# Routing steps between attention pairs: moved into the burst of value products, some to GpSimd and ScalarE

## The chip, the cores and the metric

The kernel runs on one core of a Trainium2 chip. The metric is the device time of one launch in microseconds (us). Engines have these names: PE is TensorE (PEld its weight loads), DVE is VectorE, ACT is ScalarE, POOL is GpSimd, SP is SyncE, from whose queue most DMAs are issued. Each engine works through its own instructions in order and waits on semaphores of the others.

## The reference, cut to what matters

The output is attention, then a first mixture of experts that routes each token by its largest logit, then a second one with a fixed capacity. All the edits lie in the attention and in the first routing.

```python
q_n, k_n = rmsnorm(q, g_q), rmsnorm(k, g_k)            # batch 4, 12 heads, 448 rows, 64 wide
attn = exp(scores - rowmax)
attn = attn / (sum(attn) + 1e-09)
x = (attn @ v).transpose(0, 2, 1, 3).reshape(1792, 768)
logits = x @ w_gate + modality_bias[modality_id]       # 8 experts
e_idx = argmax(logits)
gate_w = max probability, denominator + 1e-09
out[e_idx == e] = gate_w * (relu(x @ w1[e]) @ w2[e])
```

## The kernel before, in words

**Attention as a pipeline of steps.** Two heads make a pair; there are 6 pairs to a batch and 24 in all, each of 8 steps (head h, block c of 112 query rows). `attention` is a loop over steps, and an order written out by hand: the engines run what the loop emits in that order. In a step, `s1` makes the scores of one block (two products into `sp`, L230 and L231) and DVE takes their negated row maximum `nm` (L232); `s1e` lets ACT take the exponential `e` and its row sum `sm` (L238); `s2`, three steps behind (LAG1 = 3), turns a block of `e` on PE into `tp` (L246) and copies it to `et` on ACT (L252), or on DVE (L249) for two blocks of eight. Once in a pair, in the step that the code calls the burst, `s3` runs the pair's 8 value products (16 matmul records of line L259, `op`). `s4` copies `op` to `ot` and takes the reciprocal `rs` of the row sums plus 1e-9 (L273, L274); `s5` turns the result back into rows and makes the gate logits (L286, into the bank `fpt`); `s6` scales them into `xp` (L294) and `ul` (L301). `xp` goes to DRAM as rows of `xs`.

The normed inputs of the next pair are prepared beside this: POOL squares and halves (`sq`, L110 and two L114, in two halves of a group, in pairs of odd number), DVE sums (L116), POOL takes the root (L140 to L143) and scales the rows (`xn`, L167), PE turns them into columns (`pt`, L188), ACT and DVE split them (`cut`, L192 to L199), SP copies them into `at` and `bt` (L205, L207) and POOL a part into `qz` (L209).

**Routing of a batch.** When a batch's last pair is done, `emit_batch` gives a generator: `choose` sums the logits over heads (`lg`, L583), adds the bias (L585), takes the maximum (`mx`, L588), the one-hot `oh` of the first maximum (lines L502 to L510, DVE), its bfloat16 copy `ohb` (L592), and the gate: `ex` (L595, exponential on ACT L597) and the values `tr` (L601 to L609). `place` multiplies `ohb` on PE with a triangle and ones (8 small products, L619 to L623, into `fpt`) and takes from them each token's place `pl` in its expert (L629 to L635). After the third batch `star` finds the fullest expert, SP loads its number, and the weights w1 of that expert are fetched (`raws`) and split. `drip()` stands behind most DVE instructions of a step and emits the next step of `drops` (root steps) or, if there is none, of `thin` (the routing generator): several routing steps a pipeline step.

**The first slot.** `slot0` (started in step K0 = 170) finds 128 tokens of the fullest expert, fetches their rows from `xs` with one indirect DMA (L1462, tile `x`), waits some steps and turns the six column blocks on PE (L1467), split by ACT and DVE (L1469, L1471). Their first products are `pg` (L969 to L971). `extra` holds one other DMA, of the routing table `l2` to `y` (L1477).

Of the kernel before, what the change touches and what calls it, by code (L numbers as in the profile page):

```python
# [10 lines left out]
F32 = mybir.dt.float32  # L11
F32R = mybir.dt.float32r
BF16 = mybir.dt.bfloat16
# [23 lines left out]
def attention(tc, q, k, v, g_q, g_k, w_gate, consts, qkv, hook, emit_pair, emit_batch, extra, nb=NB):  # L37
# [12 lines left out]
    with ExitStack() as ctx:  # L50
# [203 lines left out]
        def s3(i, kc):  # L254
# [3 lines left out]
            for h in range(2):  # L258
# [5 lines left out]
                    stop=kc == NC - 1,  # L264
                )

        def s4(i):
            b, j = pairs[i]
            st = state[i]
            st["ot"] = p2.tile([128, S], F32, name="ot")  # L270
            nc.scalar.activation(st["ot"], st["op"], AF.Copy)
            st["rs"] = rs = p2.tile([CP, 8], F32, name="rs")
            nc.vector.tensor_scalar(rs, st["sm"], 1e-9, None, op0=OP.add)  # L273
            nc.vector.reciprocal(out=rs, in_=rs)  # L274
            if j == 0:
                uls[b] = p2.tile([CP, NC, NH, E], F32, name="ul")
            st["xp"] = p2.tile([CP, NC, 128], F32, name="xp")

        def s5(i, half):
# [8 lines left out]
        def s6(i, half):  # L288
            b, j = pairs[i]
            st = state[i]  # L290
            xp, ul, fp = st["xp"], uls[b], st["fp", half]
            cc = slice(half * 2, half * 2 + 2)
            r4 = st["rs"][:, half * 4 : half * 4 + 4].rearrange("p (c h) -> p c h", h=2)
            nc.vector.tensor_tensor(  # L294
                out=xp[:, cc, :].rearrange("p c (h d) -> p c h d", h=2),
                in0=fp[:, :, 0:128].rearrange("p c (h d) -> p c h d", h=2),
                in1=r4.unsqueeze(3).to_broadcast([CP, 2, 2, D]),
                op=OP.mult,
            )
            drip()  # L300
            nc.vector.tensor_tensor(  # L301
                out=ul[:, cc, 2 * j : 2 * j + 2, :],
                in0=fp[:, :, 128:144].rearrange("p c (h e) -> p c h e", h=2),
                in1=r4.unsqueeze(3).to_broadcast([CP, 2, 2, E]),
                op=OP.mult,
            )
            drip()
            if half == 1:
                emit_pair(b, j, xp)
# [15 lines left out]

        def drip():

            for qu in drops, thin:
                if qu:
                    if next(qu[0], qu) is qu:  # L330
                        qu.pop(0)
                    break

        def chain(gen, step, marks):

# [34 lines left out]

        for step in range(8 * np_ + 16 + LAG1):
            i, t = divmod(step, 8)
            phase[0] = step
            if i < np_:
                if step == 1:
                    stats(1, 1, (3, 3), act=True)
                if step == 2:
                    while drops:
                        drip()
                    for x in (0, 1):  # L380
                        rows(1, x, nc.vector)
                if step == 16:
                    jobs.append(init)
                if t == 0:
                    start(i)
                    if i + 1 < np_:
                        late = 0 if i else 3
                        chain(cols(i + 1, 0), step + late, ((0, last), (1, first), (1, last)))
                        chain(cols(i + 1, 1), step + max(late + 1, CQ), ((0, last), (1, first), (1, last)))
                    if i % 2 and (i + 3) // 2 < len(groups):  # L390
                        stats((i + 3) // 2, step + 2, ST)
                t0 = 0 if i % 2 else 6
                if t in (t0, t0 + 1) and i + 2 < np_:
                    while t0 and drops:
                        drip()
                    rows(i + 2, t - t0)
                if t == (4 + LAG1) % 8 and i % 2 == (4 + LAG1) // 8 and i // 2 + 2 < len(groups):
                    load(i // 2 + 2)
            for g in first.pop(step, ()):
                next(g)  # L400
            i2, n2 = divmod(step - LAG1, 8)
            i3 = i2 - 1
            if 0 <= i3 < np_ and n2 == 4:
                s4(i3)
            if 0 <= i3 < np_ and n2 == HALF0 + 1:
                s6(i3, 0)
                if i3 == np_ - 1:
                    s6(i3, 1)
            if 0 < i3 < np_ and n2 == 1:
                s6(i3 - 1, 1)  # L410
            burst = 0 <= i3 < np_ and n2 == (1 if i3 == np_ - 1 else BURST)
            if i < np_:
                s1(i, t)
                if burst:
                    s1e(i, t)
            if burst:
                for kc in range(NC):
                    s3(i3, kc)
            if 8 * np_ <= step < 8 * np_ + FILLED:
                for _ in range(FILL):  # L420
                    nc.tensor.matmul(spare()[:, 128:384], lhsT=consts["ones"], rhs=consts["ones"].unsqueeze(1).to_broadcast([128, 2, 128]), start=True, stop=True)
            if 0 <= i2 < np_:
                s2(i2, n2)
            if i < np_ and not burst:
                s1e(i, t)
            if step < 8 + LAG1:
                warm(nc, consts, idle, 6 if step < 3 else 3)
            if step < 2:
                for _ in range(3):
                    drip()  # L430
            if 0 <= i3 < np_ and n2 == HALF0:
                s5(i3, 0)
                if i3 == np_ - 1:
                    s5(i3, 1)
            if 0 < i3 < np_ and n2 == 0:
                s5(i3 - 1, 1)
            for g in last.pop(step, ()):
                drip()
                next(g)
            drip()  # L440
            job = extra(step)
# [8 lines left out]


LAG1 = 3
BURST = 3
WARM = 88
LEFT = 16
# [4 lines left out]
EV_DVE = (1, 4)  # L460
EV_LAST = (1, 4, 5, 7)
ST = (3, 5)
HALF0, FREE = 5, (3, 4)
CQ = 3


# [48 lines left out]
class Router:  # L515
# [61 lines left out]
    def choose(self, b, ul):  # L577
# [4 lines left out]
        lg = pool.tile(shp, F32, name="lg")  # L582
        nc.vector.tensor_reduce(out=lg, in_=ul.rearrange("p c h e -> p c e h"), axis=AX.X, op=OP.add)  # L583
        yield
        nc.vector.tensor_tensor(out=lg, in0=lg, in1=self.bt[:, js, :], op=OP.add)  # L585
        yield
        mx = pool.tile([CP, NC], F32, name="mx")
# [3 lines left out]
        self.ohb = self.pool.tile(shp, BF16, name="ohb")  # L591
        nc.vector.tensor_copy(out=self.ohb, in_=oh)  # L592
        yield
        ex = pool.tile(shp, F32, name="ex")
        nc.vector.tensor_tensor(out=ex, in0=lg, in1=mx.unsqueeze(2).to_broadcast(shp), op=OP.subtract)  # L595
        yield
        nc.scalar.activation(ex, ex, AF.Exp)  # L597
        yield
        yield
        gs = pool.tile([CP, NC], F32, name="gs")  # L600
        nc.vector.tensor_reduce(out=gs, in_=ex, axis=AX.X, op=OP.add)  # L601
        yield
        nc.vector.tensor_scalar(gs, gs, 1e-9, None, op0=OP.add)
        yield
        nc.vector.reciprocal(out=gs, in_=gs)
        yield
        nc.vector.tensor_copy(out=self.tr[:, js, 1], in_=gs)
        yield
        nc.vector.tensor_tensor(out=self.tr[:, js, 2], in0=gs, in1=self.tr[:, js, 1].bitcast(F32), op=OP.subtract)  # L609
        yield  # L610

    def place(self, b, pc, free=None):
# [17 lines left out]
        nc.vector.tensor_tensor(out=nxt, in0=pc[:, w : w + E], in1=cur, op=OP.add)  # L630
        self.n += 1
        yield
        nc.vector.tensor_tensor(out=ps, in0=ps, in1=self.oh[:, js, :], op=OP.mult)
        yield
        nc.vector.tensor_reduce(out=self.pl[:, js], in_=ps, axis=AX.X, op=OP.add)  # L635
# [781 lines left out]
def front(tc, consts, rp, q, k, v, g_q, g_k, modality_id, w_gate, bias, xs, w1, w2, wt, qkv, x0, l2, y):  # L1417
# [6 lines left out]
    with ExitStack() as ctx:  # L1424
# [8 lines left out]
            st["r"] = Router(tc, consts, rp, rwork, modality_id, bias, xs)  # L1433
            return st["r"].init()

        def pair(b, j, xp):
            st["r"].store(b, j, xp)

        def batch(b, ul):
            r = st["r"]  # L1440
            yield from r.choose(b, ul)
# [17 lines left out]
        def slot0():  # L1459
            r = st["r"]  # L1460
            yield from r.first_slot(st["p"][:, : 4 * (NB - 1)])
            nc.gpsimd.indirect_dma_start(out=xg, out_offset=None, in_=xs[: (NB - 1) * S], in_offset=IndirectOffsetOnAxis(ap=r.slot0[0][:, 0:1], axis=0))  # L1462
            for _ in range(5):
                yield
            for c in range(KD):
                px = (st["spare"]() if c % 2 else st["p"])[:, :128]
# [5 lines left out]
                yield  # L1472
# [1051 lines left out]
```

## Time and profile before

| what | value |
|---|---|
| median of 3 runs | 1006.93 us (1005.2 to 1008.8) |
| the profiled execution | 1000.97 us, its span 999.3 us |
| mean granted TensorE clock | 0.987 |
| busy PE, PEld | 961.2 us (96%), 778.4 us (78%) |
| busy DVE, ACT, POOL | 672.2 us (67%), 504.3 us (50%), 301.2 us (30%) |
| chain that ended last | PE 31%, issue 2%, DMA 1%, DVE 1%, ACT 1% |

Busy shares are of the span; idle time of PE is what is left of 100%. A row of a timeline has the start, the time, engine, line and operation, the tile written and the tiles read, the count, and in square brackets how long the engine was idle before it and who ended that. [...]

### The profile page before, as it was taken

The page shows a single profiled execution, that of the slowest core. Times are in us where ns is not written, and L with a number is a line of the kernel's source. Part 1 is how long each engine was busy: PE and PEld are TensorE (multiplying, and loading weights), DVE is VectorE, ACT ScalarE, POOL GpSimd, SP SyncE. Part 2 cuts the span into 40 slices and gives each one's busy share as a digit, 9 for nine tenths or more (in the row PEclk, how much of TensorE's full clock was granted, in tenths as well). Part 3 has the DMA queues.
Part 4 walks back from the last instruction along what each step waited for, and adds up shares of the span by engine and source line. Part 5 has one row for each costly group of instructions (what it writes and reads, how often), then busy time and mean ns, then how long its engine had stood idle before and what let it go on. Part 6 is the DMA issues. An engine that isn't in the chain of part 4 may idle for free. (4 is left out here: it accounts for less than half of the span.)

```text
span 999.3 us, 19414 instructions
## 1 busy us (share of the span) xinstructions
PE 961.2 (96%) x6241; PEld 778.4 (78%) x6241; DVE 672.2 (67%) x1742; ACT 504.3 (50%) x1128; POOL 301.2 (30%) x431
## 2 busy tenths in 40 slices
PE   7999999999989999999999999899999999999996
PEld 6766667677655688888888889756767699999996
DVE  6687877877875655545474665586788887787660
ACT  5787778778775422222362122561223475576651
POOL 4777667666633130001062101100010011210100
PEclk9899999999999999999999999999999999999998
DMA  6577566567465326446641111007751386866631
GB/s 164 139 156 167 138 156 165 134 159 175 112 171 194 104 90 261 144 176 222 224 165 51 33 33 66 20 15 278 256 208 37 111 303 206 270 199 237 217 122 31
DMA packets 81039, 152.58 MB, mean 153 GB/s; under 512 B 14270, under 2 KB 53438, under 8 KB 80768
## 3 DMA queue, kind: packets, MB, share of 16 engines
q1 hardware_dynamic: 75376, 127.63, 42.8%
q0 software_dynamic: 5200, 23.33, 7.2%
q8 instruction: 54, 0.88, 0.4%
q14 instruction: 89, 0.73, 0.3%
q10 hardware_dynamic: 320, 0.00, 0.0%
HBM read 112.27 MB, written 17.44 MB: 130 GB/s over the span
## 5 line engine op out<-in xcount | busy, mean ns | idle before, releaser
L238 ACT ACTIVATE e<-sp,nm 112x448 f32<-112x448 f32 x192 | 123.4, 643 | 46.4 <-DVE nm L232 43.0
L232 DVE TENSOR_REDUCE nm<-sp 112x1 f32<-112x448 f32 x192 | 116.1, 617 | 44.9 <-PE sp L231 44.4
L246 PEld LDWEIGHTS tp<-ident,e 112*112 112x112 f32 x768 | 87.7, 136 | 42.4 <-ACT et L252 9.9
L1056 DVE CUSTOM_DVE_ANT_0 prod<-po,wgb,gt 128x384 bf16<-128x384 f32 x96 | 92.7, 965 | 37.8 <-ACT yr L1280 34.3
L246 PE MATMUL tp<-ident,e 112*112 112x112 f32 x768 | 109.2, 265 | 6.6 <-ACT et L252 6.6
L2271 PE MATMUL bank<-xx,w1h 128*128 128x448 f32 x288 | 92.5, 378 | 0.0
L252 ACT ACTIVATE et<-tp 112x448 f32<-112x448 f32 x142 | 78.3, 551 | 26.7 <-PE tp L246 26.7
L230 PE MATMUL sp<-bt,at 128*112 128x448 f32 x188 | 83.9, 446 | 0.9 <-DMA bt<-cut 0.9
L969 PE MATMUL pg<-w1h,xh 128*128 128x512 f32 x180 | 75.0, 417 | 4.4 <-ACTq L926 2.2
L992 PE MATMUL po<-w2h,hh 128*128 128x384 f32 x224 | 78.9, 352 | 0.1
L259 PE MATMUL op<-et,qkv 112*64 112x448 f32 x384 | 79.0, 554 | 0.0
L2272 PE MATMUL bank<-xx,w1l 128*128 128x224 f32 x288 | 76.5, 266 | 0.0
L2311 POOL DMA_INDIRECT out_dram<-x,ids x16 | 16.4, 1026 | 198.6 <-ACT x L2310 150.2
L993 PE MATMUL po<-w2l,hh 128*128 128x384 f32 x224 | 75.2, 336 | 0.1
L994 PE MATMUL po<-w2h,hl 128*128 128x384 f32 x224 | 75.2, 336 | 0.0
L970 PE MATMUL pg<-w1l,xh 128*128 128x512 f32 x180 | 71.3, 396 | 0.0
L971 PE MATMUL pg<-w1h,xl 128*128 128x512 f32 x180 | 71.2, 395 | 0.0
L231 PE MATMUL sp<-bt,qz 128*112 128x448 f32 x188 | 70.5, 375 | 0.0
L2303 PE MATMUL bank<-w2h,hh 128*112 128x384 f32 x192 | 66.3, 345 | 0.0
L2305 PE MATMUL bank<-w2h,hl 128*112 128x384 f32 x192 | 64.7, 337 | 0.0
L2304 PE MATMUL bank<-w2l,hh 128*112 128x384 f32 x192 | 64.7, 337 | 0.0
L1092 POOL DMA_INDIRECT y<-yr,ti x11 | 11.4, 1038 | 161.6 <-POOLq L926 119.6
(476 smaller groups left out, 2289.2 us busy)
## 6 DMA issues: line engine op xcount, KB each, us to landing
qkv<-in_moe_w_dram SPq DMA_DIRECT2D x88, 384.0 KB, 4.6
qkv<-in_moe_w_dram SPq DMA_DIRECT2D x36, 512.0 KB, 8.3
raw<-in_moe_w_dram SPq DMA_DIRECT2D x24, 512.0 KB, 6.0
bt<-cut SPq DMA_DIRECT2D x96, 112.0 KB, 2.3
at<-cut SPq DMA_DIRECT2D x96, 112.0 KB, 2.3
w1s<-in_moe_w_dram SPq DMA_DIRECT2D x12, 512.0 KB, 6.9
w2s<-in_moe_w_dram SPq DMA_DIRECT2D x16, 384.0 KB, 8.2
qkv<-in_v_dram SPq DMA_DIRECT2D x12, 448.0 KB, 6.6
```

Of the source, the lines that this page charges most:

```text
L230: nc.tensor.matmul(sp, lhsT=at[:, h, cs], rhs=bt[:, h, :], start=True, stop=False)
L232: nc.vector.tensor_reduce(out=st["nm"][:, n : n + 1], in_=sp, axis=AX.X, op=OP.max, negate=True)
L238: nc.scalar.activation(e, st.pop(("s", n)), AF.Exp, bias=st["nm"][:, n : n + 1], accum_out=st["sm"][:, n : n + 1])
L246: nc.tensor.transpose(tp[:, kc, :], e[:, kc * CP : (kc + 1) * CP], ident[:CP, :CP])
L252: nc.scalar.activation(dst, tp, AF.Copy)
L259: nc.tensor.matmul(st["op"][h * D : (h + 1) * D, :], lhsT=raws[i // 2][:, 2, 2 * (i % 2) + h, kc * D : (kc + 1) * D], rhs=st["et"][:, h, k ...
L992: nc.tensor.matmul(po[n], lhsT=hh[:, k, :], rhs=w2h[:, kk, cs], start=kk == 0, stop=False)
L993: nc.tensor.matmul(po[n], lhsT=hh[:, k, :], rhs=w2l[:, kk, cs], start=False, stop=False)
L994: nc.tensor.matmul(po[n], lhsT=hl[:, k, :], rhs=w2h[:, kk, cs], start=False, stop=kk == KF - 1)
L1056: nc.vector.tensor_tensor_reduce(out=prod, in0=y, in1=wgb[:, cs, e], scale=gt, scalar=init[:, e : e + 1] if init is not None else 0.0, op0 ...
L2271: nc.tensor.matmul(pg, lhsT=h[:, k, fs], rhs=xx[:, k].rearrange("p a c -> p (a c)"), start=k == 0, stop=False)
L2272: nc.tensor.matmul(pg[:, :CAP], lhsT=l[:, k, fs], rhs=xh[:, k, :], start=False, stop=k == KD - 1)
```

## The change

- Routing steps of `thin` are no longer emitted by `drip()` while pairs run. `trickle()` emits one at the end of each step, and five in the burst step, behind the value products.
- The bias stands in `ul` as a thirteenth head (copied there by POOL, `fill`), so the sum over heads includes it and its own addition is gone. `ul` has one buffer.
- For the first three batches `ohb` is made by ACT, `ex` by POOL; the gate's later steps are a generator of their own, `gate`, which waits QUIET = 5 steps, with its constant on ACT and `tr` on POOL. The places are multiplied and summed on POOL (`fold`, three additions). The last batch keeps DVE.
- `place` may emit its products in one phase of eight (FREE) and not two.
- The row sums' constant is added by ACT in the burst step (`totals`), for every pair, and DVE takes the reciprocal alone.
- The turning of the first slot's rows begins 9 steps (LANDS) behind the gather, not 5, and takes two steps a block, not three. The DMA of the routing table is emitted in step 37, not 33.

```diff
+        def totals(i):
+            st = state[i]
+            st["rs"] = p2.tile([CP, 8], F32, name="rs")
+            nc.scalar.activation(st["rs"], st["sm"], AF.Copy, bias=1e-9)
+
         def s4(i):
...
-            st["rs"] = rs = p2.tile([CP, 8], F32, name="rs")
-            nc.vector.tensor_scalar(rs, st["sm"], 1e-9, None, op0=OP.add)
-            nc.vector.reciprocal(out=rs, in_=rs)
+            nc.vector.reciprocal(out=st["rs"], in_=st["rs"])
             if j == 0:
-                uls[b] = p2.tile([CP, NC, NH, E], F32, name="ul")
+                uls[b] = p2.tile([CP, NC, NH + 1, E], F32, name="ul", bufs=1)
...
-            for qu in drops, thin:
+            for qu in (drops, thin) if phase[0] >= 8 * np_ else (drops,):
...
+        def trickle():
+
+            if thin and phase[0] < 8 * np_ and next(thin[0], thin) is thin:
+                thin.pop(0)
...
             if burst:
+                totals(i3)
                 for kc in range(NC):
                     s3(i3, kc)
+                for _ in range(THIN):
+                    trickle()
...
             drip()
+            trickle()
...
+QUIET, THIN, LANDS = 5, 5, 9
...
-HALF0, FREE = 5, (3, 4)
+HALF0, FREE = 5, (4,)
...
+    def fill(self, b, ul):
+
+        self.tc.nc.gpsimd.tensor_copy(out=ul[:, :, NH, :], in_=self.bt[:, b * NC : (b + 1) * NC, :])
...
-        nc.vector.tensor_tensor(out=lg, in0=lg, in1=self.bt[:, js, :], op=OP.add)
...
+        if b == NB - 1:
+            nc.vector.tensor_copy(out=self.ohb, in_=oh)
+            yield
+            nc.vector.tensor_tensor(out=ex, in0=lg, in1=mxb, op=OP.subtract)
+            yield
+            yield from self.gate(b, ex, nc.vector)
+            return
+        nc.scalar.activation(self.ohb, oh, AF.Copy)
+        nc.gpsimd.tensor_tensor(out=ex, in0=lg, in1=mxb, op=OP.subtract)
+        jobs.append(self.gate(b, ex, nc.gpsimd, QUIET))
+        yield
...
+        if b < NB - 1:
+            nc.gpsimd.tensor_tensor(out=ps, in0=ps, in1=self.oh[:, js, :], op=OP.mult)
+            self.fold(self.pl[:, js], ps)
+            yield
+            return
...
-            for _ in range(5):
+            for _ in range(LANDS):
                 yield
...
                 nc.vector.tensor_tensor(out=xl[:, c, :], in0=px, in1=xh[:, c, :].bitcast(F32), op=OP.subtract)
-                yield
...
-            if i == 33:
+            if i == 37:
```

The order of the instructions at three places follows. The first is DVE's order from the step before the burst to the step behind it, when the first batch is routed; `req`, `rtm` and `oh` are the steps of the one-hot. Before:

```order
L232 TENSOR_REDUCE nm<-sp 112x1
L504 TENSOR_TENSOR req<-req,er 112x32
L507 TENSOR_REDUCE rtm<-req 112x4
L116 TENSOR_REDUCE ss<-sq 112x2x8
L510 TENSOR_TENSOR oh<-req,rtm 112x32
L232 TENSOR_REDUCE nm<-sp 112x1
L592 CAST ohb<-oh 112x32
L595 TENSOR_TENSOR ex<-lg,mx 112x32
L273 TENSOR_SCALAR rs<-sm 112x8
L274 RECIPROCAL rs<-rs 112x8
L232 TENSOR_REDUCE nm<-sp 112x1
```

And now the same steps of DVE in the changed kernel:

```order
L232 TENSOR_REDUCE nm<-sp 112x1
L116 TENSOR_REDUCE ss<-sq 112x2x8
L613 TENSOR_REDUCE mx<-lg 112x4
L232 TENSOR_REDUCE nm<-sp 112x1
L515 TENSOR_TENSOR req<-lg,mx 112x32
L517 TENSOR_TENSOR req<-req,er 112x32
L520 TENSOR_REDUCE rtm<-req 112x4
L523 TENSOR_TENSOR oh<-req,rtm 112x32
L277 RECIPROCAL rs<-rs 112x8
L232 TENSOR_REDUCE nm<-sp 112x1
```

The row maximum of the burst step stands ahead of the one-hot now, and the four steps of the one-hot stand together behind it; the copy `ohb`, `ex` and the constant of `rs` have left DVE.

The second place is ACT's order at the same burst; `e` twice are the exponentials of the two steps that end with the burst step. Before:

```order
L238 ACTIVATE e,sm<-sp,nm 112x448 x2
L252 ACTIVATE et<-tp 112x4x112
L271 ACTIVATE ot<-op 128x448
L597 ACTIVATE ex<-ex 112x32
L238 ACTIVATE e,sm<-sp,nm 112x448
```

And now on ACT:

```order
L238 ACTIVATE e,sm<-sp,nm 112x448 x2
L270 ACTIVATE rs<-sm 112x8
L623 ACTIVATE ohb<-oh 112x32
L252 ACTIVATE et<-tp 112x4x112
L276 ACTIVATE ot<-op 128x448
L238 ACTIVATE e,sm<-sp,nm 112x448
```

Two instructions have come in between the exponentials and the copy `et`, and the second of them reads what DVE makes last in the burst.

The third place is PE's order around the products of `place` for the same batch, which read `ohb`. Before, they stood at the end of the following burst step, ahead of the value products:

```order
L246 MATMUL tp<-ident,e 112x112 x4
L230 MATMUL sp<-bt,at 112x448
L231 MATMUL sp<-bt,qz_135 112x448
L619 LDWEIGHTS ut
L619 MATMUL fpt<-ohb,ut 128x32
```

And now on PE:

```order
L259 MATMUL op<-et,qkv_86 64x448 x8
L246 MATMUL tp<-ident,e 112x112 x4
L230 MATMUL sp<-bt,at 112x448
L231 MATMUL sp<-bt,qz_136 112x448
L246 MATMUL tp<-ident,e 112x112 x4
L658 LDWEIGHTS ut
L658 MATMUL fpt<-ohb,ut 128x32
```

They stand one step behind the burst in which the one-hot is made, ahead of that step's successor's score products.

## Rows read from the trace of the kernel before

**Rows 1.** Stretches from burst to burst, and the rest behind attention
```profile
96.28:107.67 11.39, 11.39 (x82) 8.31 (x81) 8.35 (x19) 9.64 (x28) 7.51 (x9) 1.00 0.92 222
72.31:84.81 12.50, 11.61 (x81) 8.33 (x80) 8.38 (x19) 10.02 (x28) 7.54 (x9) 1.00 1.07 210
107.67:123.29 15.62, 13.50 (x89) 9.75 (x88) 14.05 (x38) 9.87 (x28) 10.89 (x21) 0.89 0.35 80
180.96:196.46 15.50, 13.38 (x89) 9.91 (x89) 14.12 (x38) 9.79 (x28) 10.77 (x21) 0.89 0.35 84
254.13:268.42 14.29, 12.17 (x89) 8.51 (x88) 13.61 (x37) 9.31 (x27) 9.64 (x19) 1.00 0.37 84
350.00:975.00 625.00, 617.01 (x3911) 525.28 (x3910) 409.74 (x1055) 252.80 (x479) 90.50 (x104) 1.00 0.46 158
```

**Rows 2.** Waits of PE from 20 to 350 us: total, times, longest
```profile
PE tp L246 <- ACT et L252: 6.6, 4, 2.1
PE fpt L1467 <- DMA x<-xs,xi: 3.4, 1, 3.4
PE pg L969 <- ACT e L238: 1.3, 1, 1.3
PE sp L230 <- DMA bt<-cut: 0.9, 1, 0.9
```

**Rows 3.** Timeline of DVE from 106.5 to 116 us
```profile
109.57 0.18 DVE L502 TENSOR_TENSOR req<-lg,mx 112x32 f32<-112x32 f32 x1
...
110.20 1.35 DVE L504 TENSOR_TENSOR req<-req,er 112x32 f32<-112x32 f32 x1
111.59 0.19 DVE L507 TENSOR_REDUCE rtm<-req 112x4 f32<-112x32 f32 x1
111.69 0.41 DVE L116 TENSOR_REDUCE ss<-sq 112x16 f32<-112x256 f32 x1
112.02 0.89 DVE L510 TENSOR_TENSOR oh<-req,rtm 112x32 f32<-112x32 f32 x1
112.83 0.61 DVE L232 TENSOR_REDUCE nm<-sp 112x1 f32<-112x448 f32 x1
```

**Rows 4.** Timeline of POOL in the same pair
```profile
109.61 1.90 POOL L110 TENSOR_TENSOR sq<-qkv 112x1024 f32<-112x1024 f32 x1
111.59 2.07 POOL L114 TENSOR_TENSOR sq<-sq 112x512 f32<-112x512 f32 x2
```

**Rows 5.** Timeline of ACT in the same pair
```profile
113.54 0.64 ACT L238 ACTIVATE e<-sp,nm 112x448 f32<-112x448 f32 x1 [2.43 <-DVE nm L232]
...
114.16 0.53 ACT L252 ACTIVATE et<-tp 112x448 f32<-112x448 f32 x1
...
115.01 0.24 ACT L597 ACTIVATE ex<-ex 112x32 f32<-112x32 f32 x1
```

**Rows 6.** Timeline of PE: the stall of the same pair
```profile
114.75 0.60 PE L246 MATMUL tp<-ident,e 112*112 112x112 f32 x4 [2.12 <-ACT et L252]
```

**Rows 7.** Timeline of PE behind a burst without routing
```profile
96.28 3.23 PE L259 MATMUL op<-et,qkv 112*64 112x448 f32 x16
...
100.59 0.44 PE L230 MATMUL sp<-bt,at 128*112 128x448 f32 x1
```

**Rows 8.** Timeline of DVE in a pair without routing, burst at 84.81
```profile
86.81 0.42 DVE L116 TENSOR_REDUCE ss<-sq 112x16 f32<-112x256 f32 x1 [1.26 <-POOL sq L114]
...
87.68 0.98 DVE L273 TENSOR_SCALAR rs<-sm 112x8 f32<-112x8 f32 x1
```

**Rows 9.** Timeline of PE at the gathered rows
```profile
296.76 0.30 PE L1467 MATMUL fpt<-ident,x 128*128 128x128 f32 x1 [3.44 <-DMA x<-xs,xi]
...
297.52 4.73 PE L259 MATMUL op<-et,qkv 112*64 112x448 f32 x16
```

**Rows 10.** The tile bt from 285 to 310 us: its DMA issues and their landing
```profile
L205 SPq DMA_DIRECT2D bt<-cut x4: 462/530/876, 294.3 to 296.9; - x4
...
DMA to landing us min/median/max: 4.6/5.2/5.6
```

More of the change, by code (lines that the diff above doesn't have):

```diff
@@ L308, in s6 @@
             if half == 1:
-                emit_pair(b, j, xp)
+                emit_pair(b, j, xp, ul)
                 del state[i]
@@ L575, in store, with fold, choose @@
         self.tc.nc.sync.dma_start(out=self.xs[b * S : (b + 1) * S, 128 * j : 128 * j + 128].rearrange("(p c) d -> p c d", c=NC), in_=xp)
-    def choose(self, b, ul):
+    def fill(self, b, ul):
+        self.tc.nc.gpsimd.tensor_copy(out=ul[:, :, NH, :], in_=self.bt[:, b * NC : (b + 1) * NC, :])
+    def fold(self, out, x):
+        eng, t = self.tc.nc.gpsimd, self.work.tile([CP, NC, E // 2], F32, name="fold")
+        eng.tensor_tensor(out=t, in0=x[:, :, : E // 2], in1=x[:, :, E // 2 :], op=OP.add)
+        eng.tensor_tensor(out=t[:, :, 0:2], in0=t[:, :, 0:2], in1=t[:, :, 2:4], op=OP.add)
+        eng.tensor_tensor(out=out, in0=t[:, :, 0], in1=t[:, :, 1], op=OP.add)
+    def choose(self, b, ul, jobs):
         nc, pool, c = self.tc.nc, self.work, self.c
@@ L582, in choose @@
         lg = pool.tile(shp, F32, name="lg")
+        ex = pool.tile(shp, F32, name="ex")
+        mx = pool.tile([CP, NC], F32, name="mx")
+        mxb = mx.unsqueeze(2).to_broadcast(shp)
+        self.ohb = self.pool.tile(shp, BF16, name="ohb")
         nc.vector.tensor_reduce(out=lg, in_=ul.rearrange("p c h e -> p c e h"), axis=AX.X, op=OP.add)
         yield
-        nc.vector.tensor_tensor(out=lg, in0=lg, in1=self.bt[:, js, :], op=OP.add)
-        yield
-        mx = pool.tile([CP, NC], F32, name="mx")
         nc.vector.tensor_reduce(out=mx, in_=lg, axis=AX.X, op=OP.max)
@@ L590, in choose, with gate @@
         oh = yield from first_max_onehot_steps(nc, pool, lg, mx, c["er"], "r", out=self.oh[:, js, :])
-        self.ohb = self.pool.tile(shp, BF16, name="ohb")
-        nc.vector.tensor_copy(out=self.ohb, in_=oh)
-        yield
-        ex = pool.tile(shp, F32, name="ex")
-        nc.vector.tensor_tensor(out=ex, in0=lg, in1=mx.unsqueeze(2).to_broadcast(shp), op=OP.subtract)
-        yield
+        if b == NB - 1:
[8 more added lines that the diff above has]
+        jobs.append(self.gate(b, ex, nc.gpsimd, QUIET))
+        yield
+    def gate(self, b, ex, eng, wait=0):
+        nc = self.tc.nc
+        js = slice(b * NC, (b + 1) * NC)
+        for _ in range(wait):
+            yield
         nc.scalar.activation(ex, ex, AF.Exp)
         yield
-        yield
-        gs = pool.tile([CP, NC], F32, name="gs")
+        gs = self.work.tile([CP, NC], F32, name="gs")
         nc.vector.tensor_reduce(out=gs, in_=ex, axis=AX.X, op=OP.add)
         yield
-        nc.vector.tensor_scalar(gs, gs, 1e-9, None, op0=OP.add)
+        if eng is nc.vector:
+            nc.vector.tensor_scalar(gs, gs, 1e-9, None, op0=OP.add)
+        else:
+            nc.scalar.activation(gs, gs, AF.Copy, bias=1e-9)
         yield
@@ L606, in choose @@
         yield
-        nc.vector.tensor_copy(out=self.tr[:, js, 1], in_=gs)
+        eng.tensor_copy(out=self.tr[:, js, 1], in_=gs)
         yield
-        nc.vector.tensor_tensor(out=self.tr[:, js, 2], in0=gs, in1=self.tr[:, js, 1].bitcast(F32), op=OP.subtract)
+        eng.tensor_tensor(out=self.tr[:, js, 2], in0=gs, in1=self.tr[:, js, 1].bitcast(F32), op=OP.subtract)
         yield
@@ L1434, in hook, with pair @@
             return st["r"].init()
-        def pair(b, j, xp):
+        def pair(b, j, xp, ul):
             st["r"].store(b, j, xp)
+            if j == NPAIR - 2:
+                st["r"].fill(b, ul)
         def batch(b, ul):
             r = st["r"]
-            yield from r.choose(b, ul)
+            yield from r.choose(b, ul, st["q"])
             if b < NB - 1:
@@ L1471, in slot0 @@
                 nc.vector.tensor_tensor(out=xl[:, c, :], in0=px, in1=xh[:, c, :].bitcast(F32), op=OP.subtract)
-                yield
         def extra(i):
-            if i == 33:
+            if i == 37:
                 nc.sync.dma_start(out=y[:, DM:].rearrange("(c p) e -> p c e", p=128), in_=l2[:, :NT, :])
```

## The prediction, made before the change was run

> **What bounds the kernel now.** I read the table of stretches first, then PE's waits, then the timelines at the longest of them. Behind attention PE is busy 617.0 of 625 us at full clock [rows 1]: whatever attention gives up earlier should arrive at the end, since the work there follows PE and not the clock on the wall. Inside attention an undisturbed pair takes 11.39 us and PE is busy for all of it [rows 1], so DVE, ACT or POOL instructions gain nothing by being shorter unless a wait of PE hangs on them. The waits are few [rows 2]: `tp` on `et`, 6.6 us in 4 waits; the first slot's gather, 3.4; `pg`, 1.3; and `bt`, 0.9.
>
> The pairs in which a batch is routed take 15.62, 15.50 and 14.29 us [rows 1]. In the first, DVE is behind: it reaches the row maximum of the burst step at 112.83 [rows 3], which ends at 113.44; ACT, idle for 2.43, begins the exponential at 113.54 and the copy `et`, queued behind it, at 114.16 [rows 5]; PE gets its bank back at 114.75 after 2.12 us idle [rows 6]. [...]
>
> **What makes DVE late.** L502 takes 0.18 us; L504, the same size, takes 1.35, and L510 0.89 [rows 3]. L504 ends at 111.55, just after POOL's square, which ends at 111.51; L510 ends at 112.91, inside the two halvings that run from 111.59 to 113.66 [rows 4], so the first halving ends there. A sum over the same stretch, L116, took 0.41 beside POOL. So an addition or comparison of two SBUF tiles, and also L273, which took 0.98 beside POOL [rows 8], waits for POOL's running instruction; reductions don't. [...]
>
> **Routing, part by part.** All times are from the burst's start B (107.67 in the first batch). Removed from DVE are the bias addition, `ohb`, `ex`, the constant of `rs` and the `tr` steps. The row maximum of the burst step now stands ahead of the one-hot. But two things stand in the way of reading this as the end of the stall. POOL's squares are where they were, B+1.94 to B+3.84, then the halvings from B+3.92 to B+5.99 with the first ending about B+5.2 [rows 3, 4]. And `ohb` is on ACT ahead of `et`, while PE's `place` products stand one step behind the burst. PE reaches them when it would have reached the next score product, at 100.59 - 96.28 = B+4.31 [rows 7].
>
> DVE: L116 still waits for POOL to B+2.00 (86.81 - 84.81) and ends at B+2.42 [rows 8]; `mx`, which overlaps it, and the maximum of 0.61 [rows 3] end about B+3.1. The first comparison asks then and is held to the end of the square, B+3.88, as L504 was. The product with `er` comes next, at B+3.92: at that very moment POOL starts its halving (L507, which stood in that place, and L114 both start at 111.59 [rows 3, 4]). I take it that DVE, whose request follows at once, gets through: B+4.1; `rtm` B+4.3; `oh` is held until the first halving ends, B+5.24 as L510 was. ACT starts 0.10 later (113.44 to 113.54) and takes about 0.24 (the nearest row is the exponential of the same size), PE follows 0.06 later (114.69 to 114.75) [rows 3, 5, 6]: B+5.64. PE's wait is 5.64 - 4.31 = 1.33 in place of 2.12, a gain of 0.79, three times: 2.4 us. A wait of 0.9 left no trace on the clock (the pair of 12.50 us is at 1.00 [rows 1]), one of 2.12 did in two of three cases; at 1.33 I expect no fall and add the 2.5. Queued behind `ohb` on ACT are `et` and `ot`; PE needs `et` only after `place` and a score product, 0.9 us later, so they cost nothing more. Bounds for the three stalls: from nothing gained (below) to all 6.4.
>
> Edits at nothing: the constant of `rs` on ACT (24 small instructions) lies in the burst, where ACT is idle between the exponentials and `et`; it is idle 1.75 of 11.39 us in a clean pair [rows 1], and if that cover were gone PE would be late by about 0.2 a pair. POOL's `fill`, `ex`, product, three additions and two `tr` steps are eight small instructions a batch, at the 0.24 of ACT's small one [rows 5] 2 us, on an engine idle 3.88 of 11.39 us [rows 1]; queued behind most of them are the scaled rows of the pair after the next, which can wait. At a halving's 1.04 each (2.07 / 2 [rows 4]) they would be 8.3, and those rows could come up to 4 us late a batch: I take the first, since the size is that of the small one. The removal of L273's 0.98 shortens nothing in a clean pair, since PE did not wait there.
>
> **The first slot.** The gather's wait is 3.44 us, and the burst behind it takes 4.73 us in place of 3.23 at the lower clock [rows 7, 9]: 4.94. Four steps later, behind the burst, the rows (there at 296.7 [rows 9]) are met at about 300.5, so this wait goes. What is late next is the last pair's `bt`: its four DMAs are issued from 294.3 to 296.9 and land 4.6 to 5.6 us later, about 300.1 for the two that the first score product reads [rows 10]. Without the stall the burst is at 297.52 - 3.44 = 294.08 and that product at 294.08 + 4.31 = 298.4. I put a new wait of 1.7 there; bounds 0 (they land before they are wanted) and 2.5 (all four wanted). Net 3.2.
>
> **The table's DMA** goes from ahead of `bt` to behind it. The wait of 0.9 stands in just that pair, which took 12.50 against 11.39 [rows 1, 2]; I count 0.9, bounds 0 and 1.1. `pg` waits 1.3 for a bank behind a late exponential [rows 2] and is now emitted about one turn and some filler later: 0.6, bounds 0 and 1.3.
>
> **Sum:** 2.4 + 2.5 + 3.2 + 0.9 + 0.6 = 9.6. The profiled execution would go from 1000.97 to 991.4; it lies 6.0 below the median of the runs, so the forecast in their measure is 1006.93 - 9.6 = 997.3.
>
> **Rivals.**
> 1. *POOL wins the tie.* The product with `er` is then held to B+5.24, `rtm` ends at B+5.47, `oh` is held to the end of the second halving, B+6.04, and PE starts `place` at B+6.44: a wait of 2.13, the old stall under another name, with the old clock. What stays is 3.2 + 0.9 + 0.6 = 4.7: 1002.2. For it: the start times are equal to a hundredth. Against it: L502, asked for while POOL was about to go from one instruction to the next, was through in 0.18, POOL's next one starting at 109.61 [rows 3, 4]. [...] Chance 0.30 against 0.48.
> 2. *The stall goes altogether*, if DVE's steps all pass between POOL's instructions: 6.4 + 2.5 + 4.7 = 13.6, 993.3. Against it: L504 and L510 were both held. Chance 0.10.
> 3. *The gain is not handed on*, because something behind attention is bound by transfers or by a chain off PE: about 1006. Against it: 617.0 of 625 and a DMA share of 0.46 [rows 1]. Chance 0.07.
> 4. *Slower: ACT and PE are tied to DVE.* If one more POOL square (1.90) falls ahead of the one-hot, `ohb` holds ACT's `et` and PE in all three batches: waits of 4.0 in place of 2.12, 5.7 us, and the clock falls behind the third too, 1.3. Less 4.7 that is 2.3 over: 1009. It decides from a PE wait of 3.3 us; with the slot's new wait at its upper end and a fall of the clock there it comes to about 1011.5. Against it: POOL's queue in front of the burst is unchanged. Chance 0.05.
>
> **How the numbers follow.** What a measurement can tell from no change is 0.3%, 3.0 us. The forecast and the second rival lie beyond it (0.48, 0.10, less 0.01), the first rival mostly (0.26 of 0.30): faster 0.83. The rest of the first rival, the third and a little of the fourth: same 0.12; slower 0.05. The forecast's own range is 994.5 to 1000 (routing 1.5 to 3.5, slot 2.4 to 4.9). For 8 in 10 it has to take in most of the first rival and stop short of the second's centre: 993 to 1004.
>
> **What would show it.** Right: in the three routing pairs PE waits for `ohb` by ACT, about 1.3 us, ahead of `place`, and no longer for `et`; `oh` and the first comparison on DVE are long (0.9 each) and the product with `er` short; the granted clock of those pairs is 1.00. The gather's wait is gone and a wait for `bt` or `at` of 1 to 2 us stands behind that burst; the pair with the table's DMA is about 11.5 us. Wrong: the product with `er` over 1 us (first rival); no wait of PE at `place` (second); pairs as forecast but a stretch behind 350 us longer by as much (third); waits above 3.3 us (fourth).

## The result and the profile after

The changed kernel took 992.42 us (median of 6, 990.62 to 996.66), the kernel before beside it 1005.30 (6 runs): ratio 0.9883, 95% interval 0.9848 to 0.9918. A second measurement gave 991.88 against 1003.41: 0.9875 (0.9837 to 0.9912). The forecast was 997.3; the median lies 4.9 below it, and 0.6 below the lower end of the range. Part of that is the kernel before, from whose 1006.93 (3 runs) the forecast was counted and whose median over 6 runs is 1005.30: the ratio applied to 1006.93 gives 995.2, inside the range. From profile to profile, which is how the sum was made, it is 1000.97 to 996.66, and 991.73 in the second profile of the changed kernel.

The table of stretches of the profile after, from burst to burst, answers [rows 1]: the pair that had the table's DMA and the one behind it, the three routing pairs, and the two pairs at the first slot. A row has, for each of PE, PEld, DVE, ACT and POOL, the busy time and the number of instructions, then PE's granted clock (1.00 is full speed), the DMA engines' busy share and GB/s.

```profile
72.33:83.75 11.42, 11.42 (x81) 8.31 (x80) 8.22 (x18) 9.71 (x29) 5.56 (x7) 1.00 0.80 144
83.75:100.01 16.26, 13.53 (x81) 9.63 (x80) 9.04 (x22) 9.70 (x28) 12.48 (x22) 0.90 0.55 134
111.44:124.36 12.92, 11.90 (x91) 8.61 (x90) 11.94 (x30) 9.58 (x28) 9.90 (x21) 1.00 0.47 108
181.58:194.49 12.91, 11.89 (x89) 8.60 (x88) 11.94 (x30) 9.59 (x28) 9.90 (x20) 1.00 0.42 100
251.96:264.88 12.92, 11.90 (x90) 8.61 (x89) 11.95 (x31) 9.59 (x28) 9.90 (x21) 1.00 0.40 92
277.03:289.59 12.56, 12.56 (x89) 9.18 (x88) 10.00 (x31) 10.75 (x30) 4.07 (x3) 1.00 0.62 173
289.59:302.93 13.34, 11.48 (x77) 7.93 (x76) 8.02 (x18) 11.74 (x33) 6.09 (x4) 1.00 0.64 186
```

The routing pairs are down from 15.62, 15.50 and 14.29 to 12.9, all at full clock; the slot's two from 29.85 to 25.90; the table's pair from 12.50 to 11.42. But the next pair, 11.47 before, takes 16.26. Its wait, and the one that the forecast put behind the slot, are in PE's timeline:

```profile
91.00 0.43 PE L230 MATMUL sp<-bt,at 128*112 128x448 f32 x1 [2.70 <-DMA bt<-cut]
...
295.27 0.43 PE L230 MATMUL sp<-bt,at 128*112 128x448 f32 x1 [1.14 <-DMA bt<-cut]
```

The first routing burst is at 111.44. DVE there, answering [rows 3]:

```profile
113.86 0.62 DVE L232 TENSOR_REDUCE nm<-sp 112x1 f32<-112x448 f32 x1
114.39 0.91 DVE L515 TENSOR_TENSOR req<-lg,mx 112x32 f32<-112x32 f32 x1
115.33 0.19 DVE L517 TENSOR_TENSOR req<-req,er 112x32 f32<-112x32 f32 x1
115.56 0.19 DVE L520 TENSOR_REDUCE rtm<-req 112x4 f32<-112x32 f32 x1
115.78 0.92 DVE L523 TENSOR_TENSOR oh<-req,rtm 112x32 f32<-112x32 f32 x1
```

POOL, ACT and PE at the same place:

```profile
113.36 1.89 POOL L110 TENSOR_TENSOR sq<-qkv 112x1024 f32<-112x1024 f32 x1
115.33 2.12 POOL L114 TENSOR_TENSOR sq<-sq 112x512 f32<-112x512 f32 x2
```

```profile
116.73 0.23 ACT L623 ACTIVATE ohb<-oh 112x32 bf16<-112x32 f32 x1 [1.33 <-DVE oh L523]
116.86 0.53 ACT L252 ACTIVATE et<-tp 112x448 f32<-112x448 f32 x1
```

```profile
117.01 0.18 PE L658 MATMUL fpt<-ohb,ut 112*128 112x32 bf16 x1 [1.02 <-ACT ohb L623]
```

The first comparison ends with the square, `oh` with the first halving; the product between them begins in the very hundredth in which POOL begins its halving, and gets through in 0.19. That is no chance of this one batch: in all 24 routed batches of the eight profiles that have this order, the product took 0.19.

### The profile page after: what moved, and what is told of

Read it like the earlier page. It is cut to its first block, busy times and chain, and to the rows that moved or that the text cites. A ratio compares the mean times of both kernels' runs of the same rounds, so it can differ in the third digit from the quotient of the medians.

```text
span 994.8 us, 19359 instructions
## 1 busy us (share of the span) xinstructions
PE 960.9 (97%) x6241; PEld 780.8 (78%) x6241; DVE 655.7 (66%) x1693; ACT 506.0 (51%) x1158; POOL 306.8 (31%) x456
```

## The experiments

Each experiment has a short name, which the later sections use. `y_back`, `y_later`, `psum_onehot` and `rows_early` edit the changed kernel alone. `tie_lost`, `drip_order`, `ohb_on_dve`, `place_later` and `sums_on_dve` have one edit more on top of `y_later`, the table's DMA in step 45, and are compared with it; `both` joins `y_later` and `psum_onehot`. `before_again` and `changed_again` are the two kernels unedited. A result is the median in us, then in brackets the ratio to the kernel before that was measured beside it and its 95% interval. Those medians of the kernel before run from 1000.4 to 1005.3, and the intervals reach some 3 us to either side, while most edits are worth 1 to 5 us. So what an edit is worth is read from its pairs in the profile, and the text says where the times bear it out.

### The table's DMA

`y_back`:

```diff
-            if i == 37:
+            if i == 33:
```

> The changed kernel with one edit undone: the DMA of the routing table stands in step 33 again, not 37. In the profile of the changed kernel the pair at 72.33 takes 11.42 us (12.51 before), but the next one 16.26 (11.46 before), with a wait of 2.70 for bt and a stretch at the lower clock behind it. Theory (the table's 1792 small pieces slow whatever DMA goes out beside them, and in step 37 that is the loads for a later group and then the next pair's bt): the wait of 2.70 goes, a wait of about 0.9 is back one pair earlier, the two pairs take 12.5 and 11.5, and attention is 3.7 us shorter than in the changed kernel's profile. Rival (the 2.70 was an accident of that one execution): the first pair takes 12.5, the second 11.4, and the medians are equal or 1 us worse than the changed kernel's 992.4.

990.42 (0.9876, 0.9846 to 0.9905). The pairs took 12.57 and 11.42, with a wait of 0.91 in the first: from the second burst to the last 259.2 us, 263.1 in the changed kernel. The theory's places and sizes hold. The times don't decide against the rival: the changed kernel's two ratios are 0.9883 and 0.9875. What does is how often the wait appears, at the end of this section.

`y_later`:

```diff
-            if i == 37:
+            if i == 45:
```

> The changed kernel with the DMA of the routing table in step 45, behind the next pair's bt, where the DMA engines were busy 0.07 to 0.31 of the time. Theory (what goes out beside the table's pieces is slowed): both pairs take about 11.4 us and there is no wait for bt in either; against the changed kernel's profile attention is 4.8 us shorter, and the median 0 to 4.8 below 992.4, by how many executions had the wait. Rival (accident): the same time as the changed kernel, 992.4 within 1.5, and no wait either. Second rival (the pieces only hit the next victim): a wait of 0.9 to 2.7 for at or bt one pair later, 11.44 to 16 us for that pair.

989.49 (0.9876, 0.9849 to 0.9904). The pairs took 11.43 and 11.42, and the next one 11.42: no new victim. From the second burst to the last it is 258.2 us, 4.9 less than in the changed kernel's profile. The ratio, 0.9876, is no lower than that kernel's, so the times do not confirm the 4.9. What differs shows in the same stretches of the changed kernel (first; it issues the table's DMA at 74.56) and of this one (second; at 86.54):

```profile
75.00:80.00 5.00, 5.00 (x41) 4.12 (x38) 3.24 (x8) 3.73 (x10) 1.86 (x2) 1.00 0.77 90
80.00:85.00 5.00, 5.00 (x38) 3.68 (x38) 4.08 (x9) 4.61 (x13) 1.11 (x2) 1.00 0.91 206
85.00:90.00 5.00, 3.30 (x22) 1.58 (x18) 0.70 (x2) 0.31 (x2) 4.62 (x4) 1.00 0.92 237
```

```profile
75.00:80.00 5.00, 5.00 (x39) 3.96 (x36) 3.25 (x8) 3.58 (x9) 2.04 (x3) 1.00 0.94 239
80.00:85.00 5.00, 5.00 (x38) 3.76 (x37) 4.22 (x9) 4.60 (x14) 4.23 (x4) 1.00 0.97 233
85.00:90.00 5.00, 5.00 (x37) 3.32 (x34) 2.93 (x7) 3.38 (x11) 4.64 (x5) 1.00 0.54 85
```

In the 5 us in which the table's 1792 pieces of 36 bytes go out, the DMA engines are busy 0.77 of the time and move 90 GB/s; without them 0.94 and 239. The pieces take 75.8 to 77.2, at 50 GB/s; from there to 80, with no packet under 512 bytes, it is still 90. The loads that the changed kernel issues right behind run late into the next pair's `bt`, whose four issues SP (its queue is `SPq` in these rows) takes 5.97 us for, against 3.18:

```profile
83.17 5.97 SPq L205 DMA_DIRECT2D bt<-cut  x4
```

```profile
83.31 3.18 SPq L205 DMA_DIRECT2D bt<-cut  x4
```

Why it is 90 and not 239, no run here shows. Nor does a run separate whether the pieces slow what moves beside them or only make what is queued behind them late. A wait of 2.7 to 2.9 at this place was in all four profiles with step 37 and in none of the seven with step 45, so it is no accident of one execution. In one of the four, `psum_onehot`, the profile names ACT as its releaser and not the DMA; the four issues of `bt` took 6.16 us there.

### The routing

`psum_onehot`, the one-hot in PSUM:

```diff
-        lg = pool.tile(shp, F32, name="lg")
+        if spare is None:
+            lg, eq = pool.tile(shp, F32, name="lg"), None
+        else:
+            lg, eq = [spare[:CP, a : a + NC * E].rearrange("p (c e) -> p c e", c=NC) for a in (160, 192)]
...
-        nc.gpsimd.tensor_tensor(out=ex, in0=lg, in1=mxb, op=OP.subtract)
+        nc.vector.tensor_tensor(out=ex, in0=lg, in1=mxb, op=OP.subtract)
```

> The changed kernel, but in the first three batches the sum of the logits and the products of the one-hot lie in a bank of PSUM (free columns of fpt) and not in SBUF; the difference ex goes to DVE for that, and POOL loses that one small instruction. POOL's squares and halvings are where they were. Theory (a DVE instruction with two inputs in SBUF waits for POOL's running instruction, and that alone makes the one-hot late): the first comparison and oh take about 0.2 us instead of 0.91 and 0.92, oh ends 1.4 us earlier, ACT makes ohb about 1.2 us earlier, PE's wait of 1.02 at the products of the places goes to 0 in all three batches: 3 x 1.0 = 3.1 us less, ratio to before about 0.985. Rival (these two are long for another reason, such as reading what DVE has just written, or ohb is late because of ACT's queue): 0.9 and 1.0 us stay, time as the changed kernel's 992.4 within 1.5.

DVE's one-hot in that kernel, beside a POOL square that ran from 114.24 to 116.13:

```profile
115.28 0.19 DVE L516 TENSOR_TENSOR fpt<-fpt,mx 112x32 f32<-112x32 f32 x1
115.50 0.20 DVE L518 TENSOR_TENSOR fpt<-fpt,er 112x32 f32<-112x32 f32 x1
115.74 0.19 DVE L521 TENSOR_REDUCE rtm<-fpt 112x4 f32<-112x32 f32 x1
115.96 0.19 DVE L524 TENSOR_TENSOR oh<-fpt,rtm 112x32 f32<-112x32 f32 x1
```

PE's first product of the places has no wait in front of it:

```profile
116.71 0.18 PE L662 MATMUL fpt<-ohb,ut 112*128 112x32 bf16 x1
```

0.19 in place of 0.91 and 0.92, no wait of PE, and the three pairs took 11.70 each: the theory, to the term. The time did not follow: 991.26 (0.9899, 0.9867 to 0.9932). This kernel has step 37 (17.42 us for that pair), and its mean granted clock was 0.983 in the profile. `both`, below, shows the gain in the time.

`tie_lost`:

```diff
+    if again:
+        nc.vector.tensor_reduce(out=mx, in_=lg, axis=AX.X, op=OP.max)
     yield
     nc.vector.tensor_tensor(out=eq, in0=eq, in1=er[: shp[0]].to_broadcast(shp), op=OP.mult)
```

> The table's DMA in step 45, and in the first three batches one small reduction (the maximum mx once more, 0.2 us) between the first comparison and the product with er, so that the product asks 0.2 after POOL's first halving has begun and not with it. Theory (whichever instruction asks first goes, and a product that comes behind is held for the whole of POOL's instruction): the product takes about 1.0 in place of 0.19, oh is then held to the end of the second halving, PE's wait at the products of the places is 1.9 to 2.1 in place of 1.02, and the three pairs take 13.8 to 14.0 us, up to 15.6 where the clock falls. Rival (the halving, whose two inputs are one tile, doesn't hold DVE; only the square does): the product stays at 0.2, everything is 0.2 later, pairs of 13.1.

DVE, and POOL, whose first halving began at 111.32:

```profile
111.32 0.19 DVE L517 TENSOR_REDUCE mx<-lg 112x4 f32<-112x32 f32 x1
111.42 1.19 DVE L519 TENSOR_TENSOR req<-req,er 112x32 f32<-112x32 f32 x1
...
112.87 0.55 DVE L525 TENSOR_TENSOR oh<-req,rtm 112x32 f32<-112x32 f32 x1
```

```profile
111.32 2.05 POOL L114 TENSOR_TENSOR sq<-sq 112x512 f32<-112x512 f32 x2
```

The product took 1.19, PE waited 5.3 in three (up to 1.8), and the pairs took 13.65, 13.63 and 15.37, the last with a granted clock of 0.89; 991.88 in one run. The waits and the first two pairs are 0.1 to 0.4 shorter than the theory had them. This is the case of the prediction's first rival, brought about by the edit: a tenth of a microsecond decides it. The product that began 0.10 behind the halving took 1.19 here, the one that began with it took 0.19 in the changed kernel.

`drip_order`:

```diff
-            for qu in (drops, thin) if phase[0] >= 8 * np_ else (drops,):
+            for qu in drops, thin:
...
-                for _ in range(THIN):
-                    trickle()
...
-            trickle()
```

> The table's DMA in step 45, and of the changed kernel one part undone: the routing steps are emitted one behind each DVE instruction again, so that the one-hot stands ahead of the burst step's row maximum; the moves to ACT and POOL stay. Theory (the order is what made the stall smaller: the held comparisons then delay only ohb and not the exponentials): oh is held ahead of the row maximum, PE waits 1.5 to 2.2 us in each of the three pairs for ohb or et, the clock falls in some of them, and the routing pairs take 13.4 to 15.6 us in place of 12.9; 2 to 7 us over step 45 alone, 991.5 to 996.5. Rival (what helped is that DVE was relieved of ohb, ex and the additions): the pairs stay at 12.9 within 0.3, the time at 989.5 within 1.5.

991.08 (0.9899, 0.9866 to 0.9933); pairs of 13.53, 13.51 and 13.81. Neither side as stated: without the new order 0.6 to 0.9 a pair is lost, PE's waits in a pair come to 1.25 and not to 1.5 to 2.2, and the clock stays up. In the first of these pairs PE waits twice:

```profile
111.70 0.59 PE L246 MATMUL tp<-ident,e 112*112 112x112 f32 x4 [0.76 <-ACT et L252]
112.78 0.71 PE L289 MATMUL fpt<-rmat,ot 128*112 128x144 f32 x4 [0.49 <-ACT e L238]
```

So of the 1.37 between 14.29 and 12.92, both at full clock, 0.5 to 0.8 comes from the edits that this kernel keeps (DVE relieved, the places in one phase), the rest from the order. The kept edits were not taken apart.

`ohb_on_dve`:

```diff
-        nc.scalar.activation(self.ohb, oh, AF.Copy)
+        nc.vector.tensor_copy(out=self.ohb, in_=oh)
```

> The table's DMA in step 45, and ohb made by DVE right behind oh instead of by ACT. Theory (the wait at the products of the places is set by when oh ends): DVE makes ohb about 0.1 to 0.2 earlier than ACT did, the wait is 0.8 to 1.0 in place of 1.02, the routing pairs take 12.7 to 12.9; the time is that of step 45 alone, 989.5, within 1.5. Rival (ACT is tied up by ohb, and that holds et and the exponentials): the pairs fall by more than 0.5 each, 988 or less. Second rival (the row maximum behind ohb on DVE is later and costs PE its bank): 0.3 or more longer each.

990.40 (0.9899, 0.9875 to 0.9923); pairs of 12.86, 12.89 and 13.44. As the theory has it in two batches (wait 0.98 in the first). In the third DVE's copy was itself held, behind POOL's second halving, and PE waited 1.56:

```profile
252.51 0.75 DVE L623 CAST ohb<-oh 112x32 bf16<-112x32 f32 x1
```

`place_later`:

```diff
-HALF0, FREE = 5, (4,)
+HALF0, FREE = 5, (5,)
```

> The table's DMA in step 45, and PE's products of the places one step later (their phase is 5, not 4). Theory (the wait at these products has nothing behind it): it goes, no other comes, and the three pairs take 11.7 to 11.9 us as with the one-hot in PSUM: 3 us less than step 45 alone, 986.5. Rival (ACT makes ohb ahead of et, so PE, which has two banks for tp, now waits there for et instead): a wait of 0.7 to 1.0 for et in each of the three, pairs of 12.6 to 12.9, and a time of 989 to 990. In the changed kernel et began right behind ohb, 5.42 us behind the burst's start, and PE would want its bank some 0.3 us later than the products stand now.

991.35 (0.9859, 0.9834 to 0.9883); pairs of 13.33, 13.34 and 13.33, longer than the 12.9 without the edit. The rival, and a little more: the wait only changes its name, and PE is busy for 12.25 us of the pair in place of 11.9, which isn't explained. The times don't tell the two apart (0.9859 here, 0.9876 in `y_later`, intervals overlapping).

```profile
112.00 0.60 PE L246 MATMUL tp<-ident,e 112*112 112x112 f32 x4 [1.06 <-ACT et L252]
```

### The row sums, the first slot, and both edits together

`sums_on_dve`:

```diff
-            nc.scalar.activation(st["rs"], st["sm"], AF.Copy, bias=1e-9)
+            nc.vector.tensor_scalar(st["rs"], st["sm"], 1e-9, None, op0=OP.add)
```

> The table's DMA in step 45, and the row sums' constant added by DVE again, right ahead of the reciprocal. It tests a cost put at nothing. Theory (both engines have room there): pairs of 11.42 us as with step 45 alone, L270 on DVE about 1.0 us beside POOL and 0.2 elsewhere, the same time within 1.5. Rival one (ACT's small instruction in the burst is what makes an undisturbed pair 11.42 where it was 11.39 before): 11.39 again, 0.7 us less in all. Rival two (DVE's 1.0 us beside POOL comes into the routing pairs): these are longer by 0.2 to 1.0 each.

989.99 in one run; pairs of 11.42 to 11.48, but for an early one of 12.36 (11.88 in `y_later`, 12.25 in `tie_lost`), and routing pairs of 12.90. L270 took up to 0.98 and cost nothing that shows: the theory. The 0.03 more of an undisturbed pair than before isn't from ACT's instruction.

`rows_early`:

```diff
-QUIET, THIN, LANDS = 5, 5, 9
+QUIET, THIN, LANDS = 5, 5, 5
...
+                yield
```

> The changed kernel with the first slot's turning undone: it begins 5 steps behind the gather, with three steps a block, as before. Theory (the gather lands some 5 us after PE would want its rows, whatever the attention before it does): the wait of about 3.4 for x is back ahead of a burst, the clock falls behind it or not (0 or 1.5), the wait for bt of the last pair (1.14 in the changed kernel) goes, and the wait of pg for a late exponential is back (1.3): 3 to 6 us over the changed kernel's 992.4, 995.5 to 998.5. Rival (with the routing shorter the gather starts earlier as well, and the rows are there): no wait, within 1.5 of 992.4.

995.69 (0.9938, 0.9915 to 0.9961), the theory's time, and clear of `y_back`, 990.42, measured beside the same runs of the kernel before. The wait for `x` was 2.28, not 3.4, that of `pg` 1.3:

```profile
289.74 0.30 PE L1513 MATMUL fpt<-ident,x 128*128 128x128 f32 x1 [2.28 <-DMA x<-xs,xi]
```

The wait for the last pair's `bt` was gone. The last three pairs before the last burst took 14.92, 13.81 and 10.67 against 12.56, 13.34 and 9.64, 3.9 in all.

`both`, step 45 and the one-hot in PSUM together:

> The changed kernel with two edits put together: the routing table's DMA in step 45, and the one-hot of the first three batches in PSUM. Each alone took its wait away: with step 45 the pairs 3 and 4 took 11.43 and 11.42 us and there was no wait for bt, with the one-hot in PSUM the three routing pairs took 11.70 each. Theory (the two waits have nothing to do with each other): the gains add, attention is 3.7 us shorter than with step 45 alone, and the median is 3 to 4 below that kernel's 989.5: 985.5 to 986.5, ratio to before about 0.984. Rival (the stretch behind attention gives part of it back, since its gather waits for transfers that don't come earlier): all waits in attention gone, but 988 to 989.5.

984.82 (983.74 to 986.73; 0.9848, 0.9826 to 0.9870): the fastest kernel of the study. Routing pairs of 11.70, the table's pairs 11.42 each; the second burst to the last takes 253.8 us against 258.2 with step 45 alone. That kernel's median was 4.7 higher, but beside other runs of the kernel before (ratios 0.9848 and 0.9876, intervals overlapping). `ohb_on_dve`, which also has step 45 but the one-hot in SBUF, was measured beside the same runs: no execution of the two overlaps, 989.04 to 992.68 against 983.74 to 986.73, and its attention is 4.7 us longer. The gains add.

### What is handed on

`before_again`, the kernel before:

> The kernel before, for a second look at its profile: the first execution ended at 1000.97, below all other times of it on that chip (1001.37 to 1008.8). Theory (its waits in attention are the same each time, and what varies lies in the second routing's gathers): stalls of 2.1 in the three routing pairs and of 3.4 at the first slot's rows again, attention from the first burst to the last 283.8 within 2, and a stretch behind it longer than the 677.5 of the first profile by 0 to 7. Rival (the routing stalls themselves vary, and with them the gain of the change): attention differs by over 3.

1001.26; routing pairs of 15.63, 15.44 and 14.27, waits of 6.6 for `et` and 3.7 for `x`, attention 284.9 us, and 678.1 behind it: the theory. The stalls are the same in both profiles, to 0.01 us in the routing.

`changed_again`, the changed kernel:

> The changed kernel, nothing edited, timed in the same way as the kernels with its parts undone, to see whether its wait of 2.70 for bt is in its usual executions. Three kernels with the table's DMA in step 37 showed a wait of 2.7 to 2.9 there, those with step 45 none. Theory (the wait is in nearly every execution): it is in this profile, the pair takes 15 to 17.5 us, and the time is 4 to 5.5 over that of step 45 alone (989.5, ratio 0.9876): 993.5 to 995, ratio 0.991 to 0.993. Rival (only in some): a median of 989.5 to 992, ratio 0.988 to 0.990, and single times in two clusters 4 to 6 us apart, as the first six seemed to lie (990.6 to 993.4, and 996.7 twice).

991.88 (0.9875). The wait for `bt` was there again (2.8; the pair 16.57), yet the time is the rival's, and its two clusters of times did not appear (990.04 to 993.14). How often the wait comes, and what it costs in the median, stays open. Attention was as long as in the first profile; the gain came behind it. The stretch behind the last burst took 677.1 us here and 682.2 in the first profile. The second routing's gather in the first (top) and in this one:

```profile
665.00:670.00 5.00, 4.69 (x18) 1.98 (x18) 2.28 (x14) 0.00 (x0) 1.99 (x3) 0.66 0.42 134
675.00:680.00 5.00, 5.00 (x28) 4.89 (x29) 1.72 (x11) 0.79 (x2) 0.00 (x0) 0.65 1.03 417
680.00:685.00 5.00, 5.00 (x21) 4.78 (x21) 0.23 (x3) 0.00 (x0) 0.00 (x0) 0.50 1.04 418
```

```profile
665.00:670.00 5.00, 4.69 (x17) 2.00 (x18) 2.12 (x14) 0.00 (x0) 2.00 (x3) 0.66 0.44 133
...
675.00:680.00 5.00, 5.00 (x43) 5.00 (x42) 2.10 (x13) 0.79 (x2) 0.00 (x0) 1.00 1.02 415
680.00:685.00 5.00, 5.00 (x31) 4.72 (x30) 3.69 (x17) 1.09 (x2) 0.00 (x0) 1.00 1.03 412
```

The same work runs partly at a granted clock of 0.50 behind a wait for `xg` of 1.45 in the one, and at full clock behind 1.1 in the other. In the twelve profiles of kernels with the changed attention this stretch took 677.1 to 684.5, in the two of the kernel before 677.5 and 678.1. On average it is 3.2 longer in the twelve, and PE's waits there for `xg` sum to 1.1 to 4.2 in them, 1.1 and 1.6 in the two. So in some executions the prediction's third rival, a gather bound by transfers behind attention, takes part of the gain. Several of these profiled executions lay above their kernel's median (by up to 5.6), so that this average is not that of the usual execution.

## Why the prediction came out as it did

| gain in us | forecast | first profile after |
|---|---|---|
| three routing stalls | 2.4 | 3.3 (3 x 1.10) |
| clock falls behind two of them | 2.5 | 2.5 |
| first slot, less the wait for `bt` | 3.2 | 3.95 |
| table's DMA | 0.9 | 1.08 - 4.79 = -3.7 |
| `pg` | 0.6 | 1.04 |
| not forecast: routing pairs | 0 | 0.8 |
| not forecast: pair before the slot's two | 0 | 0.73 |
| not forecast: other pairs | 0 | 0.6 |
| attention | 9.6 | 9.3 |

That attention came out at 9.3 where 9.6 was forecast is luck: one term was wrong by -4.6, and several errors of the other sign made up for it. The mechanism of the routing, half of the sum, was right.

**Routing** went as worked out, step by step. From the burst's start: first comparison done at 3.86 (forecast 3.88), product at 4.08 (4.1), `oh` at 5.26 (5.24), PE at 5.57 (5.64). PE reached the products of `place` at 4.55, not 4.31, since one more `tp` stands ahead of them; so the wait was 1.02, not 1.33. That the long comparison and `oh` make the wait is shown by psum_onehot (0.19 in place of 0.91 and 0.92, no wait), that the order of asking decides by tie_lost (1.19 for the product behind the halving, 0.19 with it). The tie itself, to which the prediction's first rival gave 0.30, fell to DVE in 24 of 24 batches; why, no run shows. 0.27 more a pair, also gained, is PE's busy time (12.17 to 11.90 in the third) and isn't explained. The 1.04 that the prediction takes for a halving is the mean of two unequal ones, 1.27 and 0.72; nothing in its sum hangs on that. That `et`, queued behind ACT's `ohb`, costs nothing more held only because PE stood at `place` meanwhile: place_later shows it 1.06 late.

**The clock**: the forecast's 2.5 is what the first two routing pairs of the kernel before, at 0.89, took more than the third, at 1.00 [rows 1], 1.33 and 1.21; its 6.4 for all stalls is three of 2.12. Behind the first of these stalls the granted clock was 0.66 from 115 to 120 us and 1.00 again from 120 to 125. In the runs it stayed at 1.00 in the three pairs in each kernel that waited 1.0 to 1.3 there, and behind the 1.56 of ohb_on_dve; tie_lost, at 1.8, lost it in one of three, the old 2.12 in two. It fell behind the 2.70 for `bt`, too (0.90), but not behind the 2.94 of rows_early at the same place (1.00), so the length of the wait alone does not tell.

**The slot**: gather's wait gone, 1.14 in place of 1.7 for `bt`, and the pair before, with the late `ul` gone, another 0.73. Of the 5.0 that slot and `pg` gained, rows_early gives back 3.9; the rest, with the wait for `x` down to 2.28 there, comes with the other edits.

**The failed step** is "I count 0.9, bounds 0 and 1.1". It looked only at where the DMA stands in SP's queue, and took for granted that behind `bt` nobody would mind it. The DMA engines moved 50 GB/s while its pieces went out in step 37 and 90 in the 2.8 us behind them, and in two of its three places what came next was late: in step 33 that pair's `bt` (0.9), in step 37 the loads of a later group and through them the next pair's `bt` (2.70), in step 45 nothing that PE waits for. The bound below nothing was missing, 4.8 of it in the profile.

**Handed on**: in the second profile all of it (991.73, 9.2 below the first profile of before), in the first 4.8 less, through the clock behind the second routing's gather. Why it falls there in some executions and not in others stays open. Medians moved by 12.9 and 11.5 where profiles moved by 4.3 and 9.2: the kernel before, with profiles at 1000.97 and 1001.26, had medians of 1000.4 to 1005.3 in five measurements, and the two beside the changed kernel were 1005.3 and 1003.4. The two profiles lie 2.2 to 4.3 us below those two; so by estimate 2 to 4 us of the 12.9 and 11.5 are the spread of the kernel before, which no single profile shows.

## What to carry to other kernels

Where an engine's long instruction holds another's short ones, as POOL's square of 1.89 held the first comparison here (0.91), read who asks first at each place; with an operand in PSUM the comparison took 0.19. A DMA is not only a place in a queue: count its pieces (1792 here, at 50 GB/s, where 239 went without them), and look at what moves beside it where it goes. A wait that is taken away at one reader may be only the first of two: look at what is queued behind the late instruction before moving its reader.

## What the runs showed of the hardware that was not expected

A copy of one SBUF tile on DVE was held beside POOL too: in ohb_on_dve the 112x32 cast took 0.75 in one batch and 0.18 in the other two. (That a constant's addition to one tile was held, the prediction had read from L273; L270's took 0.98 at most against 0.24 in the median.) In psum_onehot the instructions of DVE whose first input is in PSUM were not held at all (0.19 to 0.20 beside a square of 1.89).
